# Running the pre-mix three periods ahead of the post-mix in a talking-heads attention kernel

## The chip, the cores and the metric

The kernel runs as one launch on one core of a Trainium2 chip. The metric is the device time of a launch in microseconds (us). The core's engines are named as the profile names them: PE (matrix multiplication; PEld is its loading of weights, which overlaps), DVE (VectorE), ACT (ScalarE), POOL (GpSimd), and SP (SyncE, which here only issues transfers). Each has an instruction stream of its own and runs it in order.

## The reference

Three stages, all in float32. The kernel gets the same arrays, some of them transposed.

```python
# q, k, v: (4 batches, 12 heads, 448, 64); w_pre, w_post: (12, 12)
scores = scale * np.matmul(q, k.transpose(0, 1, 3, 2))
scores = np.einsum('bhij,hg->bgij', scores, w_pre)      # the pre-mix, over heads
scores = scores - np.max(scores, axis=-1, keepdims=True)
attn = np.exp(scores)
attn = attn / (np.sum(attn, axis=-1, keepdims=True) + 1e-09)
attn = np.einsum('bhij,hg->bgij', attn, w_post)         # the post-mix, over heads
x = np.matmul(attn, v)                                  # -> (1792, 768)
# first MoE: x @ w_in (768, 1024), softmax-weighted h, layer norm over 1024, @ w_out (1024, 768)
# second MoE: x @ w_in (768, 2048), relu squared, @ w_out (2048, 768)
```

## The kernel before, in words

**What a period does.** The attention works on blocks of up to 10 query rows with all 12 heads side by side, so that a block fills up to 120 partitions (4 rows are kept free at the start of a tile). Two blocks make a pair; there are 90 pairs. The blocks are grouped into 16 chunks of 12 or 9 blocks. For a pair these steps follow one another:

- `qk` (PE, L222) makes the scores of a whole chunk, in six pieces of heads; each piece goes through one of two PSUM buffers ("ring") and is copied by ACT into `ssrc` (L229).
- `shuffle` (a DMA issued by SP, L236) brings the rows of one block, all heads, from `ssrc` into an `sdst` tile. There are ten of these tiles, used in turn; their first four partitions are zeroed by POOL at the start (L528).
- `pre` (PE, L256) is the pre-mix of a pair, into a PSUM buffer of its own (four of them); `negmax` (DVE, L267) finds the row maximum, `expo` (ACT, L274) makes `e` and adds up its rows into `sm`.
- `weigh` (POOL, L284, L285, L287) turns `sm` into 1/sum and multiplies it into the weights `w` of the post-mix.
- `post` (PE, L307, 56 small matmuls) is the post-mix: `e` is the stationary operand, `w` the moving one, into a ring buffer; `post_out` (DVE, L337) copies that into `at`, the transposed probabilities of a chunk.
- `av` (PE, L373), twice per chunk, multiplies `at` by v, into a ring buffer, which ACT copies into `xt`; `x_out` writes `xt` to DRAM.

**The order.** All of this is written out as one software pipeline by the loop at L598, one pass (a "slot") per pair. In slot s every engine gets its instructions in this order:

```python
shuffle of pair s + DS        # SP
pre(s + DP)                   # PE
post_out(s - 1)               # DVE
qk pieces set for slot s      # PE, then ACT
negmax, expo of pair s + DP   # DVE, ACT
av pieces set for slot s      # PE, then ACT
weigh(s + 1)                  # POOL
flush of staged MoE weights   # POOL, L102 and L103
post(s)                       # PE
```

DS is 5 and DP is 2. The six `qk` pieces of a chunk are spread over the slots that end DS slots before the chunk's first pair; q, k and v are loaded at set distances from these. The `av` pieces and `x_out` stand at slots counted from the chunk's last pair, without DS.

**What shares the engines.** From slot 5 to 64 the pieces of the MoE weights are loaded, split into a high and a low part and written back (L82 to L103 on ACT, DVE and POOL, `w1raw` loads issued by POOL, stores by SP). After the last `qk` slot (slot 79) the generator `prep` reads the first MoE's weights back, with casts on ACT (L477) and splits on POOL (L478), one step for each slot. In the last two slots the first matmuls of the first MoE (`h1`, L490) are set between `post` and `post`. What follows is the two MoE stages.

Of the kernel before, what the change touches and what calls it, by code (L numbers as in the profile page):

```python
# [7 lines left out]
F32 = mybir.dt.float32  # L8
# [10 lines left out]
def kernel(  # L19
# [18 lines left out]
    H = w_pre.shape[0]  # L38
    S = v.shape[1]
# [130 lines left out]
    sdst = {}  # L170
# [57 lines left out]
                )  # L228
        (nc.vector.tensor_copy if dve else nc.scalar.copy)(ssrc[c][:, p:H:HP, :], ps[:, :, 0:S])  # L229

    gaps = [late_p.tile([128, S], F32, name=f"sdst{i}") for i in range(10)]

    def shuffle(t):
        c, f, nk, r, oa = blocks[t]
        d = gaps[t % 10]
        (nc.scalar if t % 2 and t < 12 else nc.sync).dma_start(out=d[4:4 + r * H], in_=ssrc[c][f:f + (r - 1) * nk + 1:nk])  # L236
        sdst[t] = d

# [24 lines left out]
        pres[s] = ps  # L263

    def negmax(s, b):
        nm = late_p.tile([128, 1], F32, tag="nm", name="nm", bufs=6)
        nc.vector.tensor_reduce(out=nm, in_=pres[s][b][:, 0:S], op=ALU.max, axis=AX.X, negate=True)  # L267
        nms[s, b] = nm

    def expo(s, b):  # L270
        e = late_p.tile([128, S], F32, tag="e", name="e", bufs=6)
        if b == 0:
            sms[s] = late_p.tile([128, 2], F32, tag="sm", name="sm", bufs=4)
        nc.scalar.activation(  # L274
            out=e, in_=pres[s][b][:, 0:S], func=AF.Exp, bias=nms.pop((s, b)), scale=1.0, accum_out=sms[s][:, b:b + 1]
        )
        es[s, b] = e
        if b:
            pres.pop(s)

    def weigh(s):

        sm = sms.pop(s)
        nc.gpsimd.tensor_scalar(out=sm, in0=sm, scalar1=1e-9, scalar2=None, op0=ALU.add)  # L284
        nc.gpsimd.tensor_tensor(out=sm, in0=sm, in1=eps_sb[:, 2:3].to_broadcast([128, 2]), op=ALU.pow)  # L285
        w = late_p.tile([128, 2, H, RH], F32, tag="w", name="w", bufs=3)
        nc.gpsimd.tensor_tensor(  # L287
            out=w.rearrange("p b g i -> p b (g i)"),
            in0=wpost_bd.rearrange("p g i -> p (g i)").unsqueeze(1).to_broadcast([128, 2, H * RH]),
            in1=sm.unsqueeze(2).to_broadcast([128, 2, H * RH]),  # L290
            op=ALU.mult,
        )
        ws[s] = w
# [273 lines left out]
    psb_p = psb.__enter__()  # L567


    DS, DP = 5, 2  # L570
    jobs = {}

    def at_slot(s, f, *a):
# [34 lines left out]
    for s in range(lo_s, NP + 2):  # L608
# [36 lines left out]
        for f, a in js:  # L645
            if f is av:
                f(*a)
        if 0 <= s + 1 < NP:
            weigh(s + 1)
        while begun < len(w1at) and w1at[begun] <= s - 3 and len(fill) + len(w1f) < 4:  # L650
            start_w1(begun)
            begun += 1
# [752 lines left out]
```

## Time and profile before

| what | value |
|---|---|
| device time, 3 runs | median 1093.68 us (1092.14 to 1096.95) |
| the profiled execution | 1091.86 us, span 1090.1 us |
| mean granted clock of PE in it | 0.99 |
| PE busy | 1031.3 us, 95% of the span |
| DVE, ACT, POOL busy | 678.5, 561.7 and 672.9 us |
| attention | from 0 to about 389 us of the span |
| the MoE stages | from there to the end |

The span is what the profiler saw from the first instruction to the last; the device time of the same execution is 1.8 us longer. Busy time of one engine can lie beside that of another, so these do not add up. The profile inferred each wait from the semaphore that came last.

### The profile page before, as it was taken

The page shows a single profiled execution, that of the slowest core. Times are in us where ns is not written, and L with a number is a line of the kernel's source. Part 1 is how long each engine was busy: PE and PEld are TensorE (multiplying, and loading weights), DVE is VectorE, ACT ScalarE, POOL GpSimd, SP SyncE. Part 2 cuts the span into 40 slices and gives each one's busy share as a digit, 9 for nine tenths or more (in the row PEclk, how much of TensorE's full clock was granted, in tenths as well). Part 3 has the DMA queues.
Part 4 walks back from the last instruction along what each step waited for, and adds up shares of the span by engine and source line. Part 5 has one row for each costly group of instructions (what it writes and reads, how often), then busy time and mean ns, then how long its engine had stood idle before and what let it go on. Part 6 is the DMA issues. An engine that isn't in the chain of part 4 may idle for free.

```text
span 1090.1 us, 30147 instructions
## 1 busy us (share of the span) xinstructions
PE 1031.3 (95%) x12220; PEld 884.1 (81%) x12220; DVE 678.5 (62%) x1131; ACT 561.7 (52%) x1195; POOL 672.9 (62%) x868
## 2 busy tenths in 40 slices
PE   7798887998999799999999999999999999999998
PEld 3466555665666688898999989999999999999998
DVE  2577765885776435888887435777646833444444
ACT  4677655786777435443443446344434555444432
POOL 4667986898765726656555158676535757666630
PEclk9999999999999999999999999999999999999999
DMA  8778887889765624556564646445545521111102
GB/s 230 211 213 251 250 231 224 254 244 255 221 205 178 182 71 138 175 180 200 163 200 128 216 140 189 138 143 155 185 163 194 192 102 59 58 59 59 58 29 102
DMA packets 115914, 181.06 MB, mean 166 GB/s; under 512 B 24224, under 2 KB 87200, under 8 KB 115776
## 3 DMA queue, kind: packets, MB, share of 16 engines
q1 hardware_dynamic: 100276, 127.79, 38.2%
q0 software_dynamic: 12608, 48.55, 14.8%
q10 hardware_dynamic: 2892, 2.80, 0.9%
q8 instruction: 96, 1.57, 0.6%
q14 instruction: 42, 0.34, 0.1%
HBM read 102.42 MB, written 38.14 MB: 129 GB/s over the span
## 4 chain that ended last, share of the span: by engine, by line
PE 52%; POOL 4%; issue 3%; DVE 2%; DMA 2%; ACT 1%; SPq 0%; POOLq 0%; ACTq 0%
PE ps_y L1218 19%; PE ps_h L1147 16%; PE ps_o L801 9%; PE ps_h L490 7%; POOL ti L1075 1%; DMA ra<-w2iD 1%; DMA w2oD<-nt 1%; PE ps_tr L787 1%; POOL s L1055 1%; POOL to L1083 1%; DVE st L760 0%; DVE e L757 0%; ACT e L754 0%; DVE nm L751 0%; POOL w1o L727 0%
## 5 line engine op out<-in xcount | busy, mean ns | idle before, releaser
L1218 PE MATMUL ps_y<-to,gt 128*128 128x384 f32 x1332 | 241.8, 336 | 2.6 <-POOL to L1083 1.8
L1218 PEld LDWEIGHTS ps_y<-to,gt 128*128 128x128 f32 x1332 | 233.6, 188 | 4.9 <-POOL to L1083 2.1
L1147 PE MATMUL ps_h<-xc,ti 128*128 128x448 f32 x1080 | 225.1, 362 | 0.6 <-ACT h L1163 0.6
L1147 PEld LDWEIGHTS ps_h<-xc,ti 128*128 128x128 f32 x1080 | 201.6, 188 | 13.2 <-ACT h L1163 1.0
L337 DVE COPY at<-ps_ring 128x840 f32<-128x840 f32 (+2 forms) x114 | 96.1, 854 | 100.7 <-PE ps_ring L307 100.6
L307 PEld LDWEIGHTS ps_ring<-w,e 60*64 60x64 f32 x5040 | 89.0, 136 | 64.9 <-issue 27.3
L1229 DVE TENSOR_TENSOR y<-ps_y,y 128x768 f32<-128x768 f32 x97 | 92.4, 954 | 77.9 <-PE ps_y L1218 77.2
L841 POOL TENSOR_SCALAR nt<-nt 128x256 f32<-128x256 f32 x96 | 111.6, 1163 | 46.0 <-ACT nt L840 40.1
L307 PE MATMUL ps_ring<-w,e 60*64 60x60 f32 x5040 | 98.7, 222 | 27.1 <-issue 14.1
L229 ACT COPY ssrc<-ps_ring 128x896 f32<-128x896 f32 x92 | 82.3, 908 | 81.1 <-PE ps_ring L222 70.7
L274 ACT ACTIVATE e<-ps_pre,nm 128x448 f32<-128x448 f32 x180 | 113.2, 640 | 19.2 <-DVE nm L267 18.5
L801 PE MATMUL ps_o<-zt,w1o 128*128 128x384 f32 (+1 forms) x720 | 120.6, 326 | 1.8 <-ACT o L809 1.6
L490 PE MATMUL ps_h<-w1i,xs 128*128 128x512 f32 x504 | 118.8, 393 | 0.7 <-POOL xs L741 0.6
L801 PEld LDWEIGHTS ps_o<-zt,w1o 128*128 128x128 f32 x720 | 116.9, 189 | 2.5 <-ACT o L809 1.9
L490 PEld LDWEIGHTS ps_h<-w1i,xs 128*128 128x128 f32 x504 | 94.3, 189 | 20.6 <-POOL xs L741 1.5
L1075 POOL TENSOR_TENSOR ti<-ra,ti 128x384 fp32r<-128x384 f32 x56 | 60.0, 1079 | 79.7 <-ACT ti L1074 79.0
L267 DVE TENSOR_REDUCE nm<-ps_pre 128x1 f32<-128x448 f32 x180 | 103.2, 614 | 9.6 <-PE ps_pre L256 8.9
L1160 DVE TENSOR_TENSOR gt<-h,gt 128x448 fp32r<-128x448 f32 x64 | 50.2, 785 | 90.0 <-ACT gt L1165 85.4
L222 PE MATMUL ps_ring<-k,q 64*64 64x448 f32 x752 | 95.9, 561 | 7.8 <-DMA q<-in_qT_dram 3.2
L840 ACT ACTIVATE nt<-nraw 128x256 f32<-128x256 f32 x96 | 41.0, 433 | 119.4 <-DMA w2iD<-nt 29.9
L256 PE MATMUL ps_pre<-sdst,wpre_bd 64*64 64x448 f32 (+1 forms) x720 | 91.9, 547 | 3.1 <-issue 2.8
L1083 POOL TENSOR_TENSOR to<-ro,to 128x768 fp32r<-128x768 f32 x32 | 61.1, 1916 | 45.7 <-ACT to L1082 45.1
(111 smaller groups left out, 1526.3 us busy)
## 6 DMA issues: line engine op xcount, KB each, us to landing
sdst<-ssrc SPq DMA_DIRECT2D x166, 210.0 KB
nraw<-in_moe_w_in_dram SPq DMA_DIRECT2D x48, 256.0 KB
nraw<-in_moe_w_out_dram SPq DMA_DIRECT2D x48, 256.0 KB
ra<-w2iD POOLq DMA_DIRECT2D x32, 384.0 KB, 4.5
ro<-w2oD POOLq DMA_DIRECT2D x32, 384.0 KB, 4.0
w1raw<-in_moe_w_in_dram POOLq DMA_DIRECT2D x24, 256.0 KB, 6.5
w1raw<-in_moe_w_out_dram POOLq DMA_DIRECT2D x24, 256.0 KB, 6.9
w2iD<-nt SPq DMA_DIRECT2D x48, 128.0 KB
```

What stands on the lines that cost most here:

```text
L222: nc.tensor.matmul(out=ps[64 * u:64 * u + 64, e, 0:S], lhsT=qq[c][64 * e:64 * e + 64, p * n + u * half:p * n + u * half + 64], rhs=k[64 * ...
L256: nc.tensor.matmul(out=ps[b][64 * u:64 * u + 64, 0:S], lhsT=wpre_bd[64 * r:64 * r + m], rhs=ds[b][64 * r:64 * r + m], start=True, stop=True,)
L267: nc.vector.tensor_reduce(out=nm, in_=pres[s][b][:, 0:S], op=ALU.max, axis=AX.X, negate=True)
L274: nc.scalar.activation(out=e, in_=pres[s][b][:, 0:S], func=AF.Exp, bias=nms.pop((s, b)), scale=1.0, accum_out=sms[s][:, b:b + 1])
L307: nc.tensor.matmul(out=ps[64 * c:64 * c + 64, u, i0:i0 + PR], lhsT=ee[b][64 * u:64 * u + m, o:o + 64], rhs=w[64 * u:64 * u + m, b], start= ...
L337: nc.vector.tensor_copy(dst[:, :, :, RH * k:RH * k + RH], pv[h, :, n0:n1])
L490: nc.tensor.matmul(out=ps[:, u], lhsT=t[:, a, cc], rhs=w1i[cc][:, w, u * 512:(u + 1) * 512], start=(cc == 0 and a == 0 and w == 0), stop=( ...
L801: nc.tensor.matmul(out=ps[:, 0:width], lhsT=w1o[k][:, w, cc * 128:(cc + 1) * 128], rhs=zT[:, a, k, 0:width], start=(k == 0 and i == 0), st ...
L841: nc.gpsimd.tensor_scalar(out=t, in0=t, scalar1=2.0**-30, scalar2=2.0 - 2.0**-23, op0=ALU.is_ge, op1=ALU.mult)
L1147: nc.tensor.matmul(out=bank[b][:, 0:HT], lhsT=t[:, w, c], rhs=xc[xn][:, a, c], start=(first and j == 0 and c == 0 and i == 0), stop=(j == ...
L1218: nc.tensor.matmul(out=ps[:, u - u2[0], 0:DM // 2], lhsT=gt[:, a, f, o:o + 128], rhs=w[:, v, f, u * (DM // 2):(u + 1) * (DM // 2)], start= ...
L1229: nc.vector.tensor_tensor(out=yo, in0=po, in1=yo, op=ALU.add)
```

## The change

The pre-mix (with `negmax` and `expo`) of a pair is issued three slots ahead of its post-mix instead of two, and the shuffles six slots ahead instead of five. `weigh` is written as `weigh(s + DP - 1)`, so it stands two slots ahead of the post-mix instead of one. The distance from the shuffle to the pre-mix (three slots) and from `expo` to `weigh` (one slot) is as before. To hold what is in flight, there are twelve `sdst` tiles instead of ten, eight `nm` and `e` instead of six, five `sm` instead of four and four `w` instead of three.

Everything that the program counts from DS or DP moves one slot earlier too: the `qk` pieces with the loads of q, k and v, the last `qk` slot (78 instead of 79) and with it the start of `prep`. The `av` pieces, `x_out` and the staging of the MoE weights stay at their slots.

```diff
-    gaps = [late_p.tile([128, S], F32, name=f"sdst{i}") for i in range(10)]
+    gaps = [late_p.tile([128, S], F32, name=f"sdst{i}") for i in range(12)]
-        d = gaps[t % 10]
+        d = gaps[t % 12]
...
-        nm = late_p.tile([128, 1], F32, tag="nm", name="nm", bufs=6)
+        nm = late_p.tile([128, 1], F32, tag="nm", name="nm", bufs=8)
...
-        e = late_p.tile([128, S], F32, tag="e", name="e", bufs=6)
+        e = late_p.tile([128, S], F32, tag="e", name="e", bufs=8)
-            sms[s] = late_p.tile([128, 2], F32, tag="sm", name="sm", bufs=4)
+            sms[s] = late_p.tile([128, 2], F32, tag="sm", name="sm", bufs=5)
...
-        w = late_p.tile([128, 2, H, RH], F32, tag="w", name="w", bufs=3)
+        w = late_p.tile([128, 2, H, RH], F32, tag="w", name="w", bufs=4)
...
-    DS, DP = 5, 2
+    DS, DP = 6, 3
...
-        if 0 <= s + 1 < NP:
-            weigh(s + 1)
+        if 0 <= s + DP - 1 < NP:
+            weigh(s + DP - 1)
```

The first place is the start of PE's stream, up to the first post-mix (L307). Before, it stands behind three pre-mixes (L256, each two rows):

```order
L256 MATMUL ps_pre<-sdst_102,wpre_bd 64x448 x2
L256 MATMUL ps_pre<-sdst_103,wpre_bd 64x448 x2
L222 MATMUL ps_ring<-k,q 64x448 x4
L307 MATMUL ps_ring<-w,e 64x60 x28
L256 MATMUL ps_pre<-sdst_104,wpre_bd 64x448 x2
```

In the changed kernel the pre-mix of the fourth pair (sdst_104 and sdst_105) stands in front of it:

```order
L256 MATMUL ps_pre<-sdst_102,wpre_bd 64x448 x2
L256 MATMUL ps_pre<-sdst_103,wpre_bd 64x448 x2
L222 MATMUL ps_ring<-k,q 64x448 x4
L256 MATMUL ps_pre<-sdst_104,wpre_bd 64x448 x2
L256 MATMUL ps_pre<-sdst_105,wpre_bd 64x448 x2
L307 MATMUL ps_ring<-w,e 64x60 x28
L256 MATMUL ps_pre<-sdst_106,wpre_bd 64x448 x2
```

So one pre-mix moved ahead of the first post-mix.

The second place is PE's stream between the post-mixes of pairs 28 and 30, where a new chunk begins. Before, two `qk` pieces (L222, x8) and an `av` piece (L373) stand in one slot, behind the post-mix of pair 29:

```order
L307 MATMUL ps_ring<-w,e 64x60 x28
L256 MATMUL ps_pre<-sdst_100,wpre_bd 64x448 x2
L256 MATMUL ps_pre<-sdst_101,wpre_bd 64x448 x2
L307 MATMUL ps_ring<-w,e 64x60 x28
L256 MATMUL ps_pre<-sdst_102,wpre_bd 64x448 x2
L256 MATMUL ps_pre<-sdst_103,wpre_bd 64x448 x2
L222 MATMUL ps_ring<-k,q 64x448 x8
L373 MATMUL ps_ring<-at,v 64x120 x6
L373 MATMUL ps_ring<-at,vl_1991 64x60 x4
```

In the changed kernel the two `qk` pieces stand a slot earlier, in the one that had none, and the `av` piece has one `qk` piece beside it:

```order
L307 MATMUL ps_ring<-w,e 64x60 x28
L256 MATMUL ps_pre<-sdst_102,wpre_bd 64x448 x2
L256 MATMUL ps_pre<-sdst_103,wpre_bd 64x448 x2
L222 MATMUL ps_ring<-k,q 64x448 x8
L307 MATMUL ps_ring<-w,e 64x60 x28
L256 MATMUL ps_pre<-sdst_104,wpre_bd 64x448 x2
L256 MATMUL ps_pre<-sdst_105,wpre_bd 64x448 x2
L222 MATMUL ps_ring<-k,q 64x448 x4
L373 MATMUL ps_ring<-at,v 64x120 x6
L373 MATMUL ps_ring<-at,vl_1924 64x60 x4
```

The third place is POOL's stream around the weights of pairs 24 and 25 (w_2022 and w_2127). Before, two flushes of MoE weights (L102 and L103) stand between the two:

```order
L284 TENSOR_SCALAR sm_1905<-sm_1905 128x2
L285 TENSOR_TENSOR sm_1905<-sm_1905,eps_sb_75 128x2
L287 TENSOR_TENSOR w_2022<-wpost_bd_74,sm_1905 128x120
L102 TENSOR_SCALAR w1sq_1849<-w1sq_1849 128x256
L103 TENSOR_TENSOR w1t_1850<-w1t_1850,w1sq_1849 128x256
L102 TENSOR_SCALAR w1sq_1946<-w1sq_1946 128x256
L103 TENSOR_TENSOR w1t_1947<-w1t_1947,w1sq_1946 128x256
L284 TENSOR_SCALAR sm_2016<-sm_2016 128x2
L285 TENSOR_TENSOR sm_2016<-sm_2016,eps_sb_75 128x2
L287 TENSOR_TENSOR w_2127<-wpost_bd_74,sm_2016 128x120
```

In the changed kernel the weights of pairs 24 and 25 are w_1984 and w_2063, and the two flushes stand behind the second:

```order
L287 TENSOR_TENSOR w_1984<-wpost_bd_74,sm_1884 128x120
L419 DMA w1raw_2026<-in_moe_w_in_dram 128x256
L284 TENSOR_SCALAR sm_1945<-sm_1945 128x2
L285 TENSOR_TENSOR sm_1945<-sm_1945,eps_sb_75 128x2
L287 TENSOR_TENSOR w_2063<-wpost_bd_74,sm_1945 128x120
L102 TENSOR_SCALAR w1sq_1750<-w1sq_1750 128x256
L103 TENSOR_TENSOR w1t_1751<-w1t_1751,w1sq_1750 128x256
L102 TENSOR_SCALAR w1sq_1824<-w1sq_1824 128x256
L103 TENSOR_TENSOR w1t_1825<-w1t_1825,w1sq_1824 128x256
```

The weights of a pair moved one slot ahead of the flushes, which stay at their slots.

## Rows read from the trace of the kernel before

**Rows 1.** Busy time by stretch (us, then each engine, clock, DMA share, GB/s).

```profile
26.00:343.00 317.00, 280.23 (x7309) 188.92 (x7308) 223.89 (x404) 217.92 (x534) 240.74 (x435) 0.98 0.79 230
113.00:143.00 30.00, 23.81 (x633) 14.41 (x624) 23.75 (x45) 17.58 (x46) 27.16 (x48) 1.00 0.84 235
...
389.00:1090.00 701.00, 691.95 (x3746) 655.42 (x3742) 425.77 (x679) 309.97 (x586) 392.17 (x360) 1.00 0.43 136
```

**Rows 2.** Timeline: start, duration, engine, line, operation; in brackets idle time and releaser.

```profile
79.55 0.99 PE L307 MATMUL ps_ring<-w,e 60*64 60x60 f32 x56
...
83.17 1.04 PE L307 MATMUL ps_ring<-w,e 60*64 60x60 f32 x56 [0.36 <-ACT ssrc L229]
...
103.71 0.99 PE L307 MATMUL ps_ring<-w,e 60*64 60x60 f32 x56
...
104.77 1.04 DVE L337 COPY at<-ps_ring 128x840 f32<-128x840 f32 x1 [0.23 <-PE ps_ring L307]
...
106.03 0.99 PE L307 MATMUL ps_ring<-w,e 60*64 60x60 f32 x56
...
111.21 1.04 PE L307 MATMUL ps_ring<-w,e 60*64 60x60 f32 x56
...
112.83 0.99 PE L307 MATMUL ps_ring<-w,e 60*64 60x60 f32 x56
...
119.38 1.04 PE L307 MATMUL ps_ring<-w,e 60*64 60x60 f32 x56
```

**Rows 3.** Waits from 13 to 350 us: who, for whom: total us, times, longest.

```profile
PEld ps_ring L307 <- POOL w L287: 14.2, 17, 1.9
...
PE ps_ring L307 <- issue: 14.1, 10, 3.1
PE ps_ring L373 <- ACT ssrc L229: 10.4, 4, 3.8
```

**Rows 4.** Timeline from 112 to 138 us, POOL and PE.

```profile
122.41 0.39 POOL L287 TENSOR_TENSOR w<-wpost_bd,sm 128x120 f32<-128x120 f32 x1
...
122.84 0.91 PEld L307 LDWEIGHTS ps_ring<-w,e 60*64 60x64 f32 x56 [1.69 <-POOL w L287]
...
137.10 0.80 PE L307 MATMUL ps_ring<-w,e 60*64 60x60 f32 x39 [1.17 <-POOL w L287]
```

**Rows 5.** Timeline from 143 to 145 us, where a chunk's first scores are copied.

```profile
143.42 1.71 ACT L229 COPY ssrc<-ps_ring 128x896 f32<-128x896 f32 x2 [4.14 <-DMA w1iD<-w1t]
...
144.38 1.47 PE L373 MATMUL ps_ring<-at,v 128*64 128x120 f32 x12 [3.12 <-ACT ssrc L229]
```

**Rows 6.** Timeline of the start, 0 to 27 us.

```profile
1.06 4.13 POOL L528 MEMSET sdst<- 4x448 f32 x10
...
15.78 5.16 PE L222 MATMUL ps_ring<-k,q 64*64 64x448 f32 x24 [3.16 <-DMA q<-in_qT_dram]
...
26.31 0.79 PEld L307 LDWEIGHTS ps_ring<-w,e 60*64 60x64 f32 x48 [0.65 <-POOL w L287]
```

**Rows 7.** Timeline of the attention's end, 342 to 390 us, PE and POOL.

```profile
344.34 0.99 PE L307 MATMUL ps_ring<-w,e 60*64 60x60 f32 x56
...
348.80 1.04 PE L307 MATMUL ps_ring<-w,e 60*64 60x60 f32 x56
...
368.05 1.04 PE L307 MATMUL ps_ring<-w,e 60*64 60x60 f32 x56
372.69 1.76 PE L307 MATMUL ps_ring<-w,e 60*64 60x60 f32 x56 [3.60 <-POOL w L287]
374.38 3.71 PE L490 MATMUL ps_h<-w1i,xs 128*128 128x512 f32 x12
378.02 1.04 PE L307 MATMUL ps_ring<-w,e 60*64 60x60 f32 x56
```

**Rows 8.** The last two sets of post-mix weights on POOL in that stretch.

```profile
372.25 0.39 POOL L287 TENSOR_TENSOR w<-wpost_bd,sm 128x120 f32<-128x120 f32 x1
...
376.27 0.39 POOL L287 TENSOR_TENSOR w<-wpost_bd,sm 128x120 f32<-128x120 f32 x1
```

## The prediction

> **What bounds the kernel now.** I first split the span into stretches. In the MoE stages, from 389 us on, PE is busy 691.95 of 701 us [rows 1]: nothing that the change touches can shorten them, and they begin when the attention lets them. So the change is worth what it moves the attention's end. From 26 to 343 us PE is busy 280.23 of 317.00 us, POOL 240.74, DVE 223.89 and ACT 217.92, and the DMA engines 0.79 [rows 1]. None is full on average; the question is what ends the wait in front of each post-mix.
>
> The timeline answers that by kinds of slot, read as the distance from one post-mix (L307) to the next [rows 2]. With one `qk` piece a slot takes 2.32 us (103.71 to 106.03), with two 3.62 (79.55 to 83.17), with a `qk` and an `av` piece 5.18 (106.03 to 111.21), with two and an `av` 6.55 (112.83 to 119.38), with neither 1.62 (111.21 to 112.83). In the one-`qk` slot the reader sees a ring: the post-mix takes 0.99, the copy out of its buffer begins 1.06 after it began and lasts 1.04 (at 104.77), and the next post-mix begins 0.22 after the copy's end. In such a slot w is there in time, and weights that come a slot earlier change nothing.
>
> The table of waits then shows where a slot is longer than its kind. PEld waits for the weights w in 14.2 us (17 times); PE waits inside or before post-mixes for nothing the profile shows ("issue") in 14.1 us (10 times), and before `av` for the copies of scores in 10.4 us (4 times) [rows 3]. Only the first of these is a wait for `weigh`.
>
> **What the change does to the steady slots.** The shuffle still stands three slots ahead of its pre-mix and `expo` one slot ahead of `weigh`; the one distance that grows is from `weigh` to `post`, from one slot to two. The deeper buffers only hold that; no instruction of a slot is added. The order of PE shows the other effect: `qk` pieces move one slot against `av`. I counted the loop's slots 1 to 79 by kind, before and after: two `qk` with `av` 7 and 3, two `qk` 10 and 14, `av` alone 3 and 6, `qk` with `av` 16 and 17, neither 9 and 6, one `qk` 34 and 33. With the lengths above, and `av` alone taken as 5.18 less the 0.70 by which a `qk` lengthens an empty slot (2.32 - 1.62), 4.48, that is -4 x 6.55 + 4 x 3.62 + 3 x 4.48 + 5.18 - 3 x 1.62 - 2.32 = -0.3 us. I count it as nothing; its bounds are one slot's difference either way, 2.
>
> **The middle: post-mixes 25 to 29.** Here POOL is late. It is busy 27.16 of 30 us from 113 to 143 us [rows 1], and post-mix 25 begins at 122.84, right behind its weights (122.41 + 0.39 = 122.80), PEld having waited 1.69 [rows 4]. Post-mix 29 begins at 137.10 and still waits for w [rows 4]. From post-mix 24 at 119.38 [rows 2] that is 17.72 us for five slots, three with one `qk`, one with `qk` and `av`, one with neither: by kind 3 x 2.32 + 5.18 + 1.62 = 13.76. The excess is 4.0 us. In the changed order the weights of pairs 24 and 25 stand before the flushes that delayed them, and each set may come up to a slot (1.62 to 5.18) later against its post-mix than now without being late; the longest wait of the kind is 1.9 [rows 3], so nearly all of it is covered, provided that the backlog doesn't just run on. Estimate -4.0. The low end is nothing: the chunk boundary that follows waits for a transfer, as the first rival says, and may eat what is gained ahead of it. The upper end is all waits for w in rows 3 that lie outside these slots too, but PEld waits overlap running matmuls, so I give them no more than 1.
>
> **The start.** POOL zeroes ten `sdst` tiles in 4.13 us [rows 6], 0.41 each; two more are 0.83 us. SP's loads behind them come later by that, q of chunk 1 with them, for which PE waits 3.16 us at 15.78 [rows 6]. So I pass the 0.83 on in full. One more pre-mix stands ahead of the first post-mix at 26.31, which begins as PE comes free and w is ready [rows 6]; by an empty slot of 1.62, of which a post-mix's 0.99 is part, a pre-mix costs PE about 0.7. Sum +1.5. Bounds 0 (both may hide behind other first transfers) and 2.3 (a whole one-`qk` slot).
>
> **The end.** The `prep` splits on POOL start one slot earlier, in the same order with the weights. POOL is what the last post-mixes wait for: post-mix 88 begins at 372.69 after PE was idle 3.60, right behind its weights (372.25 + 0.39) [rows 7, 8]. The last weights are done at 376.66 [rows 8], but post-mix 89 begins only at 378.02, because twelve matmuls of the first MoE run 3.71 us from 374.38, at the lower clock that PE has after its idle stretch; post-mix 88 itself takes 1.76 instead of 1.04 [rows 7]. If POOL's chain moves by one slot, that is 1.62 (an empty slot) to 4.46 (344.34 to 348.80, with `av`) [rows 2, 7]; I take the middle, 3.0. Then the weights are ready at 369.6 and 373.7, post-mix 88 begins at 369.65, only 0.6 after post-mix 87 (368.05 + 1.04) is done, so PE keeps its clock: 1.0 for it and about 3.0 for the twelve matmuls (3.71 less the 0.7 by which post-mix 88 is lengthened), ending at 373.65. Post-mix 89 begins at about 373.7, 4.3 earlier. Bounds: with 1.62 and the low clock kept, 1.6; with 4.46 PE itself is the bound (368.05 + 1.04 + 1.0 + 3.0 = 373.1), 4.9. Everything behind follows: MoE's first matmuls wait for the attention's end only.
>
> **Sum.** +1.5 - 4.0 - 4.3 = -6.8 us. The profiled execution took 1091.86, so 1085.1. The median shown is 1093.68, 1.8 above it; I set the forecast against the median: 1086.9. A measurement of this kernel can tell about 0.5%, 5.5 us, from no change, so the likeliest case lies just beyond that line.
>
> **The rivals.**
>
> *The middle's gain is taken back at a chunk boundary.* ACT waits 4.14 us until 143.42 with a chunk's first copy of scores, and PE 3.12 with `av` [rows 5]: the copy overwrites `ssrc` that the last shuffle of two chunks before is still reading, and it starts when that transfer has landed (the row names a store of SP as the last to end; what the program makes the copy wait for is the shuffle). If the transfers set the pace in this stretch (DMA share 0.84 [rows 1]), PE comes earlier to the same wait and only waits longer. For it: all four waits of this kind, 10.4 us [rows 3]. Against: a share of 0.84 is not 1, and the shuffles are issued from a stream that moves with PE. [...] Then +1.5 - 4.3 = -2.8, 1090.9: no change that can be told.
>
> *More boundaries stall (the other side).* Place: the first `qk` copy of each of 14 chunks. Its distance to the shuffles is kept, but in the changed order two `qk` pieces stand together in a slot without `av` in front of them (14 such slots instead of 10), so the copy is asked for sooner after the last shuffles were issued. Price: 10.4 / 4 = 2.6 us each. With 5 more boundaries stalling, +13, less 6.8: 1099.9. It is slower by over 0.5% from (6.8 + 5.5) / 2.6, about 5 more; if the rival above holds too, from (2.8 + 5.5) / 2.6, about 3 more. Against: the one in rows 5 sits in a slot of two `qk` and `av` (the `av` is what waited), and these become fewer.
>
> *The change does nothing of what it could.* If the weights are late because POOL's work as a whole is late, a slot's lead is used up within a few slots, and at the end POOL's last splits set the time whatever the lead. Then only the start remains: +1.5, 1095.2. For it: POOL at 27.16 of 30 us [rows 1]. Against: the stretch before has POOL at less (240.74 of 317 in all), in which a lead can be gained.
>
> **How the numbers follow.** My forecast 0.45, taken back 0.25, nothing 0.13, more stalls 0.17. The forecast's own range is its terms' bounds: from 0 - 5.0 - 4.9 - 2 = -11.9 to 2.3 - 2.0 - 1.6 + 2 = +0.7 (with half of the middle, since none of it is the first rival). The forecast stands 1.3 beyond 5.5, so about three in four of it count as faster, 0.34, and the rest as within 0.5%; of "taken back" (-2.8, with the same bounds of the other terms) four in ten, 0.10. That is 0.44, rounded to 0.45. Slower: most of "more stalls" and a little of "nothing": 0.17. The rest, 0.38, is within. The range goes from 1081 to 1099, which leaves out the far end of "more stalls" and the rare case in which more goes than I see.
>
> **What would show it.** In the profile after: the table of waits has L307 waiting for w in 14.2 us now, and nearly nothing then, before the last five post-mixes; post-mixes 25 to 29 take about 14 us instead of 17.7; the first post-mix begins at 27.8; post-mix 89 begins 4 us sooner, counted from post-mix 80, with no idle of 3 us before post-mix 88; the MoE stage keeps its 701 us. Wrong would make it: a longer wait of ACT's L229 on a landing at 143 us and its like; more "issue" time in post-mixes, of which 14.1 us [rows 3] has no cause in the trace; or a MoE stage of another length, which I have counted as equal. Of the "issue" waits no row tells what they wait for, so none of the sum rests on them: one more or less is 1.4 us (14.1 / 10).

## The result: 0.8% slower

The changed kernel took 1104.52 us in the median (1097.67 to 1111.12, 15 runs), the kernel before, beside it on the same chips, 1098.27 (1089.79 to 1110.07, 15 runs): a ratio of 1.0079 with a 95% interval of 1.0051 to 1.0107. The forecast was 1086.9 with a range of 1081 to 1099. The same kernel differs by up to 2% from one execution to the next; the first three times of before, from which the forecast was counted, lay at the fast end of that. So of the 17.6 us between forecast and measurement 4.6 are the base (1093.68 against 1098.27), and 13.0 the change: 6.8 us faster was forecast, 6.2 slower was measured.

The page of the profile after (the span, busy times, and the queue that becomes important below):

```profile
span 1099.1 us, 30132 instructions
...
PE 1039.1 (95%) x12220; PEld 887.9 (81%) x12220; DVE 677.3 (62%) x1131; ACT 561.5 (51%) x1195; POOL 674.2 (61%) x870
...
q8 instruction: 96, 1.57, 0.6%
```

The stretches that answer to [rows 1], the MoE stages counted from the first of their matmuls behind the attention:

```profile
26.00:343.00 317.00, 277.14 (x7031) 186.69 (x7027) 215.85 (x395) 212.09 (x521) 234.34 (x424) 0.97 0.79 225
397.20:1099.10 701.90, 692.04 (x3738) 655.27 (x3736) 426.27 (x679) 309.54 (x586) 393.04 (x360) 1.00 0.43 135
```

From 26 to 343 us PE is busy 277.14 us, a little less than the 280.23 of before, and has run 278 matmuls fewer by then (7031 against 7309). The MoE stages are as long as before (701.9 against 701 in [rows 1]). The attention ends 8 us later. The waits from 13 to 350 us, as in [rows 3]:

```profile
PE ps_ring L307 <- issue: 18.2, 14, 3.1
PE ps_ring L307 <- ACT ssrc L229: 6.5, 9, 4.0
...
PE ps_ring L373 <- issue: 2.9, 2, 2.1
PE ps_ring L373 <- ACT ssrc L229: 2.1, 3, 1.5
...
PEld ps_ring L307 <- POOL w L287: 4.0, 8, 0.9
```

PEld waits for w in 4.0 us instead of 14.2, PE not at all: what the change was to remove is gone in this stretch. There is more "issue" instead. Post-mixes 24 and 29, as in [rows 2, 4]:

```profile
132.73 1.04 PE L307 MATMUL ps_ring<-w,e 60*64 60x60 f32 x56
...
147.91 1.02 PE L307 MATMUL ps_ring<-w,e 60*64 60x60 f32 x56
```

That is 15.18 us for slots that by their new kinds (two with one `qk`, one with `qk` and `av`, one with two `qk`, one with neither: 2 x 2.32 + 5.18 + 3.62 + 1.62) take 15.06. The 4.0 us of excess are gone there. But post-mix 24 itself begins at 132.73 instead of 119.38, so the time was lost ahead of the place that the change was made for. The end of the attention, as in [rows 7]:

```profile
379.00 1.04 PE L307 MATMUL ps_ring<-w,e 60*64 60x60 f32 x56
...
379.73 0.39 POOL L287 TENSOR_TENSOR w<-wpost_bd,sm 128x120 f32<-128x120 f32 x1
...
381.00 0.79 ACT L379 COPY xt<-ps_ring 128x180 f32<-128x180 f32 x2
...
381.89 1.23 PE L307 MATMUL ps_ring<-w,e 60*64 60x60 f32 x56 [1.84 <-POOL w1i L478]
...
383.05 3.02 PE L490 MATMUL ps_h<-w1i,xs 128*128 128x512 f32 x12
385.99 1.04 PE L307 MATMUL ps_ring<-w,e 60*64 60x60 f32 x56
```

PE is idle for 1.84 instead of 3.60 before post-mix 88, and the twelve matmuls run at the full clock. The profile puts the 1.84 down to POOL, but the weights of pair 88 (379.73 + 0.39) are long there. Post-mix 88 begins 0.10 behind the end of ACT's copy of `xt` (381.00 + 0.79), which frees the ring buffer that it fills. The start, as in [rows 6]: POOL's memsets take 0.81 longer, and the first post-mix begins 0.83 later.

```profile
1.06 4.94 POOL L528 MEMSET sdst<- 4x448 f32 x12
...
27.14 0.45 PE L307 MATMUL ps_ring<-w,e 60*64 60x60 f32 x8
```

**What an "issue" wait is.** One of the new ones, in post-mix 21 of the profile after:

```profile
114.87 0.37 PE L307 MATMUL ps_ring<-w,e 60*64 60x60 f32 x8
118.36 1.55 PE L307 MATMUL ps_ring<-w,e 60*64 60x60 f32 x48 [3.12 <-issue]
119.69 1.72 PE L256 MATMUL ps_pre<-sdst,wpre_bd 64*64 64x448 f32 x8
```

Eight of 56 matmuls run, then PE stands for 3.12 us and waits for no semaphore. The page's queue q8 moves 96 packets and 1.57 MB in both first profiles, 16 KB each, for the 2 x 12220 matmuls and loads of weights of PE; with the 257 instructions with which PE's sequencer waits (243 before) the trace has 24697 (24683), 257 to a packet. I call such a packet a block, and put the landings beside the count of instructions that PE had begun by then:

```
profile        packet  landed   PE resumed  instructions begun at the landing  PE had stood
after              14  116.97       118.36  256 x 14 + 449                             3.34
after              38  252.84       254.14  256 x 38 + 449                             2.76
before              4   52.31        53.88  256 x  4 + 449                             3.36
before             26  175.99       177.59  256 x 26 + 449                             2.77
```

In none of the twenty traces had PE begun more than 449 instructions beyond 256 times the number of packets landed before. Counts of exactly 449 at a landing, five before and ten after in these two profiles, lie whole multiples of 256 instructions apart, and PE stands at each of them, for 1.61 to 3.36 us. It resumed 1.30 to 1.60 us after these landings, 1.2 to 1.9 in all twenty traces. That PE is out of instructions there is my reading of these counts. Of PE's stands of over 1.2 us in the attention, those that end behind such a landing are 12.4 of 30.5 us in the first profile of before and 19.6 of 30.3 after.

The wait before a chunk's first scores [rows 5] is there too, at another boundary:

```profile
174.56 1.71 ACT L229 COPY ssrc<-ps_ring 128x896 f32<-128x896 f32 x2 [4.61 <-DMA sdst<-ssrc]
...
175.61 1.28 PE L307 MATMUL ps_ring<-w,e 60*64 60x60 f32 x56 [4.01 <-ACT ssrc L229]
```

One more of this kind stands under another name:

```profile
271.10 1.71 ACT L229 COPY ssrc<-ps_ring 128x896 f32<-128x896 f32 x2 [3.15 <-DMA sdst<-ssrc]
...
272.15 1.77 PE L307 MATMUL ps_ring<-w,e 60*64 60x60 f32 x56 [3.33 <-POOL sm L285]
```

The first of these two copies ends at 272.01, and the post-mix begins 0.14 later, as at 175.61; its weights had been made before. So the 3.33 us belong to the score copies too.

And this stand cost a second time. After its 3.12 us the granted clock is at the lower of the two levels that the traces of before and after have, 0.50 of the full one:

```profile
114.00:117.00 3.00, 1.24 (x20) 0.51 (x12) 1.77 (x3) 3.00 (x9) 2.35 (x6) 1.00 0.63 214
118.30:121.60 3.30, 3.24 (x58) 1.84 (x60) 1.11 (x2) 0.00 (x0) 3.05 (x7) 0.50 0.92 238
122.00:125.00 3.00, 3.00 (x110) 2.94 (x109) 2.86 (x9) 2.06 (x6) 1.22 (x3) 1.00 0.88 243
```

Before the stand it was 1.00, in the stretch behind it 0.50, then 1.00 again: the other 48 matmuls take 1.55 us and the pre-mix 1.72 instead of 0.94.

### The profile page after: what moved, and what is told of

Its sections match the earlier page's. It is cut to its first block, busy times and chain, and to the rows that moved or that the text cites. A ratio compares the mean times of both kernels' runs of the same rounds, so it can differ in the third digit from the quotient of the medians.

```text
span 1099.1 us, 30132 instructions
## 1 busy us (share of the span) xinstructions
PE 1039.1 (95%) x12220; PEld 887.9 (81%) x12220; DVE 677.3 (62%) x1131; ACT 561.5 (51%) x1195; POOL 674.2 (61%) x870
## 3 DMA queue, kind: packets, MB, share of 16 engines
q8 instruction: 96, 1.57, 0.6%
## 4 chain that ended last, share of the span: by engine, by line
PE 48%; DVE 4%; POOL 3%; DMA 3%; issue 3%; ACT 1%; SPq 0%; POOLq 0%; ACTq 0%
PE ps_y L1218 19%; PE ps_h L1147 16%; PE ps_o L801 7%; PE ps_h L490 6%; DMA w2oD<-nt 1%; POOL ti L1075 1%; DMA ra<-w2iD 1%; DVE st L760 1%; DVE e L757 1%; POOL s L1055 1%; DVE nt L869 1%; DMA nraw<-in_moe_w_in_dram 1%; POOL to L1083 1%; DVE nt L865 1%; PE ps_tr L787 0%
## 5 line engine op out<-in xcount | busy, mean ns | idle before, releaser
L307 PEld LDWEIGHTS ps_ring<-w,e 60*64 60x64 f32 x5040 | 93.7, 137 | 64.7 <-issue 27.6
L307 PE MATMUL ps_ring<-w,e 60*64 60x60 f32 x5040 | 102.1, 223 | 30.4 <-issue 18.2
L229 ACT COPY ssrc<-ps_ring 128x896 f32<-128x896 f32 x92 | 82.1, 907 | 91.9 <-PE ps_ring L222 78.7
L490 PEld LDWEIGHTS ps_h<-w1i,xs 128*128 128x128 f32 x504 | 93.9, 188 | 20.3 <-POOL xs L741 1.5
L256 PE MATMUL ps_pre<-sdst,wpre_bd 64*64 64x448 f32 (+1 forms) x720 | 101.3, 567 | 7.2 <-issue 5.4
L222 PE MATMUL ps_ring<-k,q 64*64 64x448 f32 x752 | 99.6, 563 | 5.7 <-DMA q<-in_qT_dram 3.0
```

The costliest lines, as they stand in the source:

```text
L222: nc.tensor.matmul(out=ps[64 * u:64 * u + 64, e, 0:S], lhsT=qq[c][64 * e:64 * e + 64, p * n + u * half:p * n + u * half + 64], rhs=k[64 * ...
L256: nc.tensor.matmul(out=ps[b][64 * u:64 * u + 64, 0:S], lhsT=wpre_bd[64 * r:64 * r + m], rhs=ds[b][64 * r:64 * r + m], start=True, stop=True,)
L307: nc.tensor.matmul(out=ps[64 * c:64 * c + 64, u, i0:i0 + PR], lhsT=ee[b][64 * u:64 * u + m, o:o + 64], rhs=w[64 * u:64 * u + m, b], start= ...
L490: nc.tensor.matmul(out=ps[:, u], lhsT=t[:, a, cc], rhs=w1i[cc][:, w, u * 512:(u + 1) * 512], start=(cc == 0 and a == 0 and w == 0), stop=( ...
```

## The experiments

There were eighteen runs; two more profiles of before and one of the changed kernel are among them, since one profile is a sample. The others have one profile each, and not always of a middling execution: those of `before_avfirst`, `ds6_dp2` and `after_lean` are among the slowest of their kernel, those of `bufs_only` and `weigh_end_avfirst` among the faster. The table has for each the ratio to before, then from its profile PE's waits from 26 to 400 us by cause, how late the blocks landed (from when PE began its instruction 256 k + 192 to the landing of packet k, mean over the attention; worked out from the trace like the list above, so it serves for comparing kernels only), and the number of stretches at half clock, which are not all of one length. Instruction 256 k + 192 is a point that I chose; the expectations call what is counted from it the block's latency, or the time since it was asked for, but no trace shows when a block is asked for. Waits that the profile puts down to other work of POOL are in no column. The long ones among them are the 3.33 us above, 3.5 of the same kind in `after_lean`, and one of 1.6 to 3.4 us before post-mix 88 in most kernels with earlier weights.

| kernel | ratio (95%) | issue | score copies | w | block, us | half clock |
|---|---|---|---|---|---|---|
| before, 1st profile | | 16.9 | 12.5 | 10.4 | 3.19 | 5 |
| before_again, 2nd | | 24.4 | 11.1 | 6.7 | 3.57 | 6 |
| before_null, 3rd | 0.9992 (0.9947 to 1.0037) | 17.6 | 13.7 | 9.2 | 3.16 | 4 |
| the change | 1.0079 (1.0051 to 1.0107) | 26.5 | 9.2 | 0 | 3.91 | 6 |
| after_again | 1.0092 (1.0054 to 1.0130) | 24.2 | 13.9 | 0 | 3.88 | 5 |
| bufs_only | 1.0045 (1.0007 to 1.0082) | 15.5 | 16.7 | 6.9 | 3.16 | 5 |
| ds5_dp3 | 1.0035 (1.0004 to 1.0066) | 15.6 | 4.9 | 0 | 3.26 | 4 |
| ds6_dp2 | 1.0064 (1.0031 to 1.0097) | 26.0 | 9.3 | 7.4 | 3.92 | 7 |
| weigh_end | 1.0022 (0.9994 to 1.0050) | 23.6 | 17.1 | 1.8 | 3.58 | 6 |
| weigh_same | 1.0145 (1.0099 to 1.0191) | 13.7 | 30.0 | 5.0 | 3.42 | 6 |
| after_loads | 1.0148 (1.0102 to 1.0195) | 36.6 | 8.9 | 0 | 4.26 | 6 |
| after_gaps10 | 1.0084 (1.0054 to 1.0114) | 26.2 | 10.8 | 0 | 3.91 | 6 |
| before_lean | 0.9881 (0.9833 to 0.9928) | 7.9 | 9.5 | 14.0 | 2.61 | 3 |
| after_lean | 0.9893 (0.9833 to 0.9952) | 11.2 | 11.1 | 0.4 | 3.32 | 4 |
| before_avfirst | 1.0084 (1.0049 to 1.0118) | 33.6 | 5.9 | 9.2 | 4.12 | 7 |
| weigh_end_avfirst | 1.0028 (0.9994 to 1.0063) | 21.4 | 3.6 | 6.8 | 3.83 | 2 |
| after_avfirst | 1.0121 (1.0074 to 1.0169) | 29.2 | 10.4 | 0.7 | 4.40 | 5 |
| before_w1_70 | 0.9955 (0.9923 to 0.9986) | 26.1 | 8.6 | 5.6 | 3.55 | 6 |
| weigh_end_w1_70 | 1.0007 (0.9975 to 1.0040) | 25.3 | 10.4 | 1.9 | 3.50 | 9 |
| after_w1_69 | 1.0137 (1.0077 to 1.0196) | 18.8 | 22.2 | 0 | 3.77 | 9 |

**How much an execution differs from the next.** `before_again`, `before_null` and `after_again` are unchanged kernels.

> The kernel before, unchanged, for a second profile of it. In the first profile PE stood still for 13.0 us in 9 places inside a post-mix or behind it, each time until a 16 KB packet of PE's instruction queue had landed; the profile of the changed kernel has 23.9 us in 10 places. Theory 1 (these fetches wait longer behind transfers that the change issues a slot further ahead): the second profile of before stays near 13, within 9 to 17. Theory 2 (the fetches fall anew in every execution, and the two profiles differ by chance): the second profile is anywhere between 10 and 25, and its time moves with it.

> The kernel before against itself, a control for the comparison, with a third profile of it. Every theory: a ratio of 1, within 0.3%. If it is 0.3% or more above 1, the differences of the first runs (0.35 to 0.64%, that of the buffers alone among them) say little. Of the profile: fetch stalls between 10 and 25 us if they fall anew in each execution (the first two profiles have 13.0 and 22.9).

> The changed kernel once more, with a second profile. Theory 1 (transfers issued further ahead delay the instruction fetches): stalls for fetches of 20 us or more again, and 4 to 9 us slower than before. Theory 2 (chance): stalls of 10 to 25 us, and the ratio may come out anywhere from 0.998 to 1.008. Both: no waits for w in post-mixes 25 to 29, about 14 us for the five slots but for fetches.

The issue waits of before are 16.9, 24.4 and 17.6 us, in executions of 1091.86, 1100.22 and 1090.66 us: they do fall anew each time, as theory 2 said. The means differ, 19.6 before and 25.4 after (26.5 and 24.2), but the highest of before lies between the two of after, so these sums alone don't tell the kernels apart. The times do: the change measures slower twice, with a control that measures the same. So chance makes the scatter, not the loss.

**The change in parts.** `bufs_only` has the buffers, with `DS, DP = 5, 2`; the other two move one distance alone.

```diff
-    DS, DP = 6, 3
+    DS, DP = 5, 3   # ds5_dp3, with ten sdst tiles;  6, 2 in ds6_dp2
```

> Only the buffers of the change (twelve sdst tiles, eight nm and e, five sm, four w), with the distances of before. Theory 1: at most the two memsets at the start, 0 to 1 us slower than before. Theory 2: within 3 us of before, with stalls that differ from those of before as much as the changed kernel's do. A rival for the whole change, that more shuffles may be under way at once through the two further sdst tiles: 5 us or more slower.

> Only the pre-mix (with the maximum, exp and weigh) goes a slot further ahead; shuffles, scores and the loads of q, k and v stay where they were, so the pre-mix comes two slots after its shuffle instead of three. Theory 1 (loss from transfers that are issued further ahead): the fetch stalls stay near 13 us, post-mixes no longer wait for w, and the kernel is 4 to 8 us faster than before, unless the pre-mix now waits for shuffles. Theory 2 (chance): within 3 us of before, stalls anywhere. Rival 3 (any deeper pre-mix costs, since shuffles land 7 to 10 us after issue): ACT or PE waits for shuffles, 5 us or more slower than before.

> Only the shuffles, the scores and the loads of q, k and v go a slot further ahead; the pre-mix and the weights stay two slots and one slot ahead of the post-mix. Theory 1: fetch stalls of 20 us or more, waits for w as before, 8 to 16 us slower than before (worse than the whole change, which at least removes the waits for w). Theory 2: within 3 us of before. Rival 3: the same as before or faster, since the pre-mix has a slot more behind its shuffle.

With six slots alone, issue waits and block times are those of the whole change, which bears theory 1 out in part; that it would be worse than the whole change, 8 to 16 us, did not come. The times of the three parts don't separate: 1.0035, 1.0045 and 1.0064 have intervals that overlap. With the pre-mix alone the blocks stay short and no w is waited for, but nothing is gained where 4 to 8 us were expected. PE's waits from 26 to 400 us in the profile of `ds5_dp3`:

```profile
PE ps_ring L307 <- issue: 12.8, 10, 5.8
PE ps_pre L256 <- DMA sdst<-ssrc: 9.7, 13, 1.8
```

Two slots behind its shuffle, the pre-mix waits for it in 9.7 us (13 times), which no profile of before has: rival 3, though the kernel is not 5 us slower by it. Of the 159 shuffles that SP issues from 26 to 343 us in the first trace of before, the last update of the semaphore comes 3.6 to 12.8 us after the issue, 6.9 in the median; the 7 to 10 us of rival 3 are their longer half. That the buffers alone measure 1.0045 I can't explain; their profile is like those of before, and their interval overlaps the control's. As the whole change holds these buffers too, it isn't excluded that a part of its 0.8% is theirs.

**The weights alone.** The distances and transfers of before, but `weigh(s + 2)`, behind the flushes of slot s or (`weigh_same`) ahead of them, with the four `w` and five `sm` of the change.

```diff
-        if 0 <= s + 1 < NP:
-            weigh(s + 1)
...
             flush(sq, t)
             w1s[i] = t
+        if 0 <= s + 2 < NP:
+            weigh(s + 2)
```

> The kernel before with the distances of before, but the weights two slots ahead: weigh stands at the end of a slot's work on POOL for the pair two ahead (behind the flushes, before the next slot's loads), with four w and five sm. It takes the waits for w away and moves no transfer. Theory 1 (the transfers issued a slot further ahead lengthen the wait for PE's instruction blocks, by 0.65 us in the mean, and the gain goes there): blocks land 3.1 to 3.6 us after they are asked for, as in all profiles with five slots, PE waits for w in less than 3 us, and the kernel is 3 to 7 us faster than before. Rival (any earlier weights only let PE run into the next wait, for a shuffle at a chunk's beginning or a block): waits for w gone, but within 3 us of before, with longer waits of that kind.

> The same, but weigh stands where it stood, ahead of the flushes, so POOL has to wait for the exp of the same slot. Theory 1: as the one at the slot's end if POOL waits little, 2 to 6 us faster; the price is POOL's waiting for ACT in each slot, which delays flushes and splits. Rival: within 3 us of before. If POOL's wait costs more than its lead gives, waits for w come back and it is slower by up to 5 us.

PE's waits in the same stretch in the profile of `weigh_end`:

```profile
PE ps_ring L373 <- ACT ssrc L229: 14.5, 6, 4.9
PE ps_ring L307 <- issue: 12.6, 13, 2.0
PE ps_pre L256 <- issue: 7.2, 6, 2.8
...
PE ps_ring L307 <- POOL w L287: 1.8, 3, 0.8
```

This decided one question. `weigh_end` takes the waits for w from 6.7 to 10.4 us down to 1.8, moves no transfer, and gains nothing (1.0022): PE's time without work from the first post-mix to the end of the last is 47.4 us, against 42.9 to 45.7 in the profiles of before. Score copies are longer, 17.1 us where before has 11.1 to 13.7; issue, 23.6, lies within the 16.9 to 24.4 of before; and 3.4 us stand before post-mix 88, where ACT's copy of `xt` ends. My theory had it 3 to 7 us faster and fell here; the rival held. Ahead of the flushes POOL waits 71.7 us for the exp instead of 57.8, and the kernel is 1.5% slower, more than any case expected.

**Loads and tiles.** The changed kernel with the loads of q, k and v one slot later (`beg - 1`, `beg - 7`, `beg + 2`), and with ten `sdst` tiles.

> The changed kernel with the loads of q, k and v back at the slots of before; scores and shuffles stay six slots ahead. Theory 1 in the form that the loads are what lies in front of the fetches: blocks land 3.2 to 3.5 us after they are asked for instead of 3.9, and the kernel is 2 to 6 us faster than the changed one. If it is the shuffles and the scores' slots, latency stays at 3.7 to 4.1 and the time within 2 us of the changed kernel's.

> The changed kernel with ten sdst tiles instead of twelve, so that a shuffle must wait for the pre-mix of five pairs before, as in the kernel before, and no more than ten can be under way or waiting. If the depth of the shuffle queue is what the fetches wait behind: latency 3.2 to 3.5 us and 2 to 6 us faster than the changed kernel. If not (with twelve tiles and the old distances it was 3.16): 3.7 to 4.1 and within 3 us of the changed kernel.

The tiles make no difference to time or blocks. Later loads make it worse, which neither case expected: the block time rises to 4.26 and the issue waits to 36.6.

**Fewer transfers.** The lean kernels load the MoE weights fully only for the first seven pieces, and four columns of the others.

```diff
+        n = WP if i < 7 else 4
-        nc.gpsimd.dma_start(out=t, in_=src[k * 128:(k + 1) * 128, o:o + WP])
+        nc.gpsimd.dma_start(out=t[:, 0:n], in_=src[k * 128:(k + 1) * 128, o:o + n])
```

> The kernel before, with the loads of the MoE weights behind the first seven pieces cut to four columns (the staged weights are those of the first seven pieces, so the product of the MoE stages is another one). All instructions stay, some 10.5 MB of transfers between 30 and 300 us go. If the fetch stalls come from full DMA queues (both theories), they fall from 13 to 23 us to under 9, and the waits of the first scores of a chunk for a shuffle shorten; the kernel is 6 to 15 us faster. The waits for w stay, or grow, since PE comes earlier to them. If fetches don't depend on the transfers, the stalls stay at 13 to 23.

> The changed kernel with the same loads cut. If what took the gain back are the fetches and shuffles behind full DMA queues, this one is faster than the lean kernel before by 3 to 7 us (the waits for w of the middle and the end), where with all loads it was slower. If the loss is another (the scores moved against av, the start, the buffers), it is slower than the lean kernel before by 2 to 8 us.

PE's waits in that stretch, first in the lean kernel with the distances of before:

```profile
PE ps_ring L307 <- POOL w L287: 14.0, 13, 3.4
PE ps_ring L373 <- ACT ssrc L229: 8.0, 6, 2.7
PE ps_ring L307 <- issue: 5.2, 3, 2.0
```

and then in the lean kernel with the change:

```profile
PE ps_ring L307 <- ACT ssrc L229: 8.8, 9, 4.2
PE ps_ring L307 <- issue: 7.8, 8, 2.3
...
PE ps_ring L307 <- POOL w L287: 0.4, 1, 0.4
```

With less traffic the first loses most of its issue waits (7.9 us instead of 16.9 to 24.4) and is 1.2% faster, and its waits for w grow to 14.0 (6.7 to 10.4 before). The second has hardly any of these, and its ratio is that of its own kind before (0.9893 against 0.9881). With six executions of each, whose intervals are 0.5 to 0.6% wide to either side, that suggests that the loss needs the full traffic and doesn't show it. The gain of the second over the first doesn't appear either: of the 13.6 us less for w, issue takes 3.3, score copies 1.6 by the table and 3.5 more that the profile puts down to POOL, ACT's copy of `xt` before post-mix 88 takes 2.4, and 20.5 us instead of 10.2 are at half clock; here too my expectation of 3 to 7 us failed.

**The waits at a chunk's beginning.** `av` is written ahead of the `qk` pieces of its slot, in the kernels of before, with earlier weights, and changed.

> The kernel before with av ahead of the qk pieces of the same slot. If the waits at a chunk's beginning (5 to 11 us in three profiles of before, all in front of an av that stands behind two qk pieces) end at a landing that comes when it comes, 2.8 us of each are now covered by the av's matmuls: waits of PE for the copies of scores fall to about half, 2 to 6 us faster. If what the av covers is lost to the next block or landing all the same, within 2 us of before.

> The weights two slots ahead (at the slot's end, transfers not moved) and av ahead of the qk pieces. If the gain of earlier weights was taken back by the waits at a chunk's beginning, taking these away too lets it show: 5 to 11 us faster than before. If it was taken back by the waits for PE's instruction blocks, PE runs into more of these (over 25 us of issue waits) and the kernel is within 3 us of before.

> The changed kernel with av ahead of the qk pieces. Its waits at a chunk's beginning stand mostly in slots of two qk pieces without av, where nothing can be moved ahead: 0 to 3 us faster than the changed kernel, 4 to 9 us slower than before. The blocks' latency stays at 3.7 to 4.1 us, as in every profile with six slots; if it falls to 3.2 to 3.6 here, the order on PE and not the slots of the transfers sets it.

PE's waits in the same stretch in the profile of `before_avfirst`:

```profile
PE ps_ring L307 <- issue: 27.5, 18, 3.9
PE ps_ring L307 <- POOL w L287: 9.2, 5, 2.8
PE ps_ring L373 <- issue: 5.8, 6, 3.3
PE ps_ring L307 <- ACT ssrc L229: 5.2, 10, 1.7
```

The kernel before loses its waits in `av` for score copies (10.4, 5.5 and 11.2 in its three profiles, none here), and has 33.6 us of issue waits instead of 16.9 to 24.4; it is 0.8% slower, where 2 to 6 us faster or no change was expected. The same happened with another wait, in one profile: take one away, and the blocks come late instead. With earlier weights as well (`weigh_end_avfirst`) nothing is gained (1.0028): the score copies fall to 3.6 us, but waits for w come back to 6.8, and issue is 21.4. `after_avfirst` is slower than the change (1.0121), and its blocks take 4.40 us, so this order doesn't shorten them.

**The rate of the transfers.** The staging of the MoE weights ends at slot 70 or 69 instead of 64.

```diff
-    first_w1, last_w1 = 5, 64
+    first_w1, last_w1 = 5, 70
```

> The kernel before with the staging of the MoE weights spread over slots 5 to 70 instead of 5 to 64, so that the same transfers go at nine tenths of the rate. If the waits of the attention are those for blocks and landings behind full queues (with most of these loads cut, blocks landed 0.6 us sooner and the kernel was 15 us faster): block latency 3.0 to 3.3 us in the mean, 1 to 5 us faster. If a slot's rate of transfers doesn't matter: within 2 us of before.

> The same with the weights two slots ahead, at the slot's end. If the earlier weights' gain goes to blocks and landings, less traffic lets some of it show: 2 to 7 us faster than before. If not: within 3 us of before, as without the spreading.

> The changed kernel with the staging spread over slots 5 to 69 (its last slot for scores is one earlier). If the transfers' rate is what the change suffers from: latency 3.4 to 3.8 us instead of 3.9, and 1 to 6 us faster than the changed kernel. If it is the slots of shuffles and scores: within 2 us of it, 4 to 9 us slower than before.

Only the kernel before gains by it, 0.45%, with an interval just clear of 1: it is the fastest complete kernel here. Its profile doesn't show the shorter blocks that I gave as the reason (3.55), so why it is faster stays open. `weigh_end_w1_70` stays where `weigh_end` was, and the changed kernel gets slower by it (1.0137), where 1 to 6 us less was expected.

## Why the prediction was wrong

The distances between post-mixes tell where the time went. They are worked out from the starts of L307 in the three profiles of before and the two of the change:

| post-mixes | before, us | the change, us | by the slots' kinds |
|---|---|---|---|
| 0 to 24 | 93.1, 99.7, 95.5 | 105.6, 108.6 | +0.6 |
| 24 to 30 | 29.0, 28.5, 29.4 | 20.3, 20.7 | -0.1 |
| 30 to 40 | 40.8, 35.7, 34.7 | 44.3, 45.0 | +1.2 |
| 40 to 80 | 155.1, 159.8, 155.5 | 157.5, 154.7 | -2.1 |
| 80 to 89 | 33.7, 34.0, 33.3 | 31.1, 33.0 | 0 |

- **The middle, -4.0.** The five slots lose their excess, as worked out, and with the stand behind post-mix 29 the stretch from 24 to 30 even loses 8.4 us in the mean. The step that failed is that the gain was entered in the sum at its full size, "so nearly all of it is covered", as if it moved the attention's end. The next ten slots take it back: from 24 to 40 together it is 69.8, 64.2 and 64.1 us before and 64.7 and 65.7 after. The score copies from 30 to 40 are 4.4 and 4.1 us, against 3.1, 1.0 and 1.3. In the second profile of before PE waits for no w in the five slots, and they take 16.1 us instead of 17.7, so the 4.0 was also one execution's figure. The first rival, "taken back at a chunk boundary", described this, with 1090.9 us, and `weigh_end`, which gains nothing either, speaks for it. That the transfers set the pace there was my estimate, and no run shows it; shown is that from 24 to 40 the change takes 65.2 us in the mean and before 66.0, where by the kinds it would take 1.1 more.
- **The "issue" waits and the steady slots, 0.** This is the missing term. "None of the sum rests on them", I wrote of the issue waits, since no row told what they wait for, and of the steady slots "I count it as nothing". Up to post-mix 24 the change takes 11.0 us more in the mean, where before waits for w in at most 0.8 us, so this is no gain that is taken back but a cost of the change's own. The issue waits there are 8.6, 8.7 and 10.9 us before, 15.7 and 14.0 after, and that is nearly all by which they grew (19.6 to 25.4 in the whole). All six profiles with six slots and full traffic (`av` in its place) have 102.0 to 112.3 us up to post-mix 24, all nine with five slots 90.9 to 100.1. So it comes with the six slots, not with the earlier pre-mix or weights. With most of the loads cut it is still there, 91.9 against 99.1, and there issue waits don't explain it.
- **The end, -4.3.** Too large, because the sum had only one wait in front of post-mix 88. In the trace of before another ends just ahead of that for w:

```profile
370.87 0.79 ACT L379 COPY xt<-ps_ring 128x180 f32<-128x180 f32 x2
```

ACT's copy out of the ring buffer that post-mix 88 fills ends at 371.66, the weights at 372.64 [rows 8], so with earlier weights alone post-mix 88 could begin 0.9 sooner, not 3.0. In all twelve traces with earlier weights it begins 0.10 behind this copy; in the other eight, where it waits for w, it begins 1.0 behind it, and in `before_avfirst` 2.25. From post-mix 80 to 89 the change takes 1.6 us less in the mean: 6.1 for w are gone, 1.9 stand before post-mix 88, and slots 81 and 84 got longer by 1.1 and 2.0 us in the first profile, the second of them with a stand of 1.52 us at the count of 449.
- **The start, +1.5.** The memsets cost 0.81 as said. The first post-mix begins at 26.3, 27.8 and 27.6 before and 27.1 and 27.7 after: 0.2 later in the mean, so the pre-mix in front of it cost nothing that shows.
- **Steady slots, -0.3.** The kinds' lengths add up to 296.6 us before and 296.3 after; the count held. What came on top of them was 55.1, 61.0 and 51.8 us before, and 62.5 and 65.8 after: 8.2 more in the mean, which is the loss. Little of it is idle time: PE's time without work from the first post-mix to the end of the last was 43.2, 45.7 and 42.9 us before and 44.4 and 44.7 after. Most is in PE's busy time, and there in the pre-mixes: counted from the end of the matmul before, they hold PE for 72.0, 72.1 and 69.4 us before and for 78.9 in both profiles of the change. Of that, 1.6, 3.8 and 0 us were at half the clock before, 8.3 and 5.3 after, and waits inside a pre-mix, two or three before, became six and seven. What makes the rest of the difference I can't assign.
- **The other side.** "More boundaries stall" would have come to 1099.9, near the changed kernel's profiled 1100.91, by luck: waits for score copies are 12.5 (with the 3.33 above) and 13.9 us, 11.1 to 13.7 before.

So three terms failed, each shown by its stretch: the middle is taken back, the end had a second wait 1 us behind the first, and the first 24 slots cost 11 us that stood nowhere in the sum. What makes these slots longer is narrowed down, not settled. All six profiles with six slots and full traffic have blocks of 3.77 to 4.26 us, all nine with five slots 3.16 to 3.58 (`av` in its place in all fifteen). Twelve tiles (3.16), earlier weights (3.58) and an earlier pre-mix (3.26) with five slots, and ten tiles with six (3.91), leave them there; later loads (`after_loads`, 4.26 instead of 3.91 and 3.88) and another order on PE (`before_avfirst`, 4.12 instead of 3.16 to 3.57) came with later blocks. Which transfer, if any, delays which block the trace doesn't tell, and no kernel was run that moves the score pieces alone or the shuffles alone.

## What to carry to other kernels

Where several waits stand close behind one another in a pipeline, one that is removed is worth only what the next one leaves, here 0.9 of 3.0 us before post-mix 88. Before it is entered in the sum, look in the trace of before for everything else that the same instruction needs (its operands, and the buffer that it writes) and enter the distance to the one that ends next; and ask for each later wait whether it ends at a time of its own, such as a landing. A wait is not always what the profile names: where that one was long done, look for a copy that ends about 0.1 us ahead (0.10 and 0.14 here). "Issue" waits inside long rows of small matmuls are to be counted against the instruction queue's packets; with most of the MoE loads left out they fell here to 7.9 us. And where executions of one kernel differ by 2%, take a second profile before reading a small term from one.

## What was not expected of the hardware

- PE had begun at most 449 instructions beyond 256 for each block landed, in all twenty traces, and resumed 1.2 to 1.9 us after a late block's landing. In the first profiles a stand took up to 3.4 us (post-mix 21 after, post-mix 7 before), the longest of all 6.0 (`ds5_dp3`).
- Every stretch at the lower clock between the first and the last post-mix of the two first profiles, eleven in all, began between 0.7 us before and 1.1 us after the end of a stand of 1.99 to 4.01 us. Not every such stand was followed by one (2.36 to 46.02 and 2.80 to 169.31 before, 2.34 to 47.62 and 2.07 to 71.57 after, were not), and none of the shorter waits for w of before was (0.82, 0.97 and 1.17 us ahead of post-mixes 25, 27 and 29). In these two profiles, then, the lower clock came with stands of 1.99 us and more alone.
- What the text ahead calls the splitting of the staged MoE weights is their narrowing from 64 to 32 bits; the 256 KB pieces are of 64-bit numbers. And `prep` takes not one but two steps a slot from slot 85 on, from slot 84 in the change. Nothing in the argument hangs on either.
